# Linear attention block: three x tiles transposed on TensorE, crossbar blocks of 2, 3, 4, 4 tiles, and a state that ends by feature block

## The chip, the cores and the metric

The kernel runs on one core of one Trainium2 chip. The metric is the device time of one execution in microseconds; lower is better.

The core has five engines with a queue each: TensorE (PE in the profile, and PEld for its weight loads), VectorE (DVE), ScalarE (ACT), GpSimd (POOL) and SyncE (SP, which here only starts DMAs). All queues run at the same time, each in its own order, and meet at semaphores.

## The reference

The input x has 2048 rows (tokens) of 640 features, in bf16. There are 32 heads of 20 features.

```python
qkv = (x @ wqkv) split into q, k, v, each [32 heads, 2048, 20]
phi = lambda t: where(t > 0, t + 1, exp(t)) + 1e-6
pq, pk = phi(q), phi(k)
kv  = einsum("bhsd,bhse->bhde", pk, v)      # per head, 20 x 20
z   = einsum("bhsd->bhd", pk)               # sum over tokens
num = einsum("bhqd,bhde->bhqe", pq, kv)
den = einsum("bhqd,bhd->bhq", pq, z) + 1e-6
out = (num / den) as [2048, 640] @ wo
```

## The kernel before

The 2048 tokens are 16 tiles of 128. The 640 features are 5 blocks of 128 (the index c or d in the code). Nothing is recomputed and everything stays in SBUF after one load.

The kernel never forms v. It uses kv = pk^T (x wv) = (x^T pk)^T wv in effect: a state x^T pk of 640 x 640 is summed over the tokens, multiplied by wv, masked to the heads' diagonal blocks, and multiplied by wo. The output is then one matmul of the normalized phi(q) with that product.

The stages are these.

- **Loads and transposes.** k and q need x with the features on the partitions (tile xT). NPE says how many x tiles are transposed on TensorE; the rest are transposed by the DMA crossbar. XCH lists the row ranges: the first NPE entries are single tiles for TensorE, the others are one crossbar DMA each, issued by `load_xT` (L181) on SP's queue. `transpose_x` (L187) does one tile on TensorE: five transposes into two PSUM banks, then one copy per bank to xT, by VectorE or ScalarE. The state matmuls use x untransposed (tile xn, loaded by `load_xn`, L224). `load_wk` (L230) issues the first loads on the SP and ScalarE queues; `load_rest` (L253) queues the q weights, the remaining x tiles, the v weights and wo behind the crossbar DMAs on SP.
- **k.** For every token tile `k_half` (L272) makes two halves of 320 columns over five feature blocks, in two of the eight PSUM banks (tile number modulo 4 picks the pair). `k_phi` (L286) applies phi: Exp on ScalarE (L290), two VectorE instructions (L292, L295), which write pk. The first tiles are interleaved with the TensorE transposes by a short string named order (L557).
- **State.** The state is made in two halves of columns, 360 and 280. In each half, `p_step` (L300) adds one token tile into five banks, 0 to 4, one per feature block of x. `p_out` (L312) copies the five banks to tile pt, by ScalarE (even blocks) and VectorE (odd blocks).
- **Beside the state.** `q_tile` (L324) makes one feature block of phi(q) for 512 tokens: five matmuls of 512 columns (L330), Exp on ScalarE (L338), and VectorE (L344, L352). A variant with `two_act` lets ScalarE do the Relu (L342), so that VectorE's last instruction reads SBUF alone (L349). VectorE sums pk over tiles (z, L358 to L385), `z_finish` (L391) sums over the partitions on TensorE, and GpSimd spreads the sums into head masks (zb, L403).
- **After each half.** `kv_group` (L407) multiplies pt by wv for three groups of 120 features, `kv_mask` (L423) keeps the heads' blocks on VectorE, and the w2 functions (L434 to L465) multiply by wo, copy with ScalarE and rearrange the rows by an SP DMA into w2p.
- **Denominators and output.** `den` (L467) and `den_act` (L482) form the reciprocals for half of the tokens as exp(-ln(den)); `den_spread` (L488) spreads them by four SP DMAs, and `normalize` (L495) multiplies phi(q) by them on VectorE. `out_tile` (L533) makes one output tile in two banks; one copy on ScalarE, one on VectorE, one DMA.

PSUM has eight banks. During the state, banks 0 to 4 hold its five sums, and the list small hands out banks 5, 6, 7 in turn to everything else. Each P.add call states what an instruction reads and writes, and waits follow from it; a p_step is one such call, so all its waits stand ahead of its first matmul.

The order of all work after k is written out by hand in a string (L646). Each letter adds the instructions of one piece, for all engines at once:

```text
p  next state step            o  copy the five banks of a half
q  next q tile                Q  the same, Relu on ScalarE
z  next sum of pk             s  z_finish
k, K  kv group of half 0, 1   0 to 5  w2 of group 0 to 5
i, I  denominators            n  next normalization
T  next output tile
```

The first state steps of tiles 0 and 1 (half 0) stand ahead of the string, and the sixteenth output tile behind it.

Of the kernel before, what the change touches and what calls it, by code (L numbers as in the profile page):

```python
# [82 lines left out]
def bass_standalone__linear_attn_block__prompt_kernel(nc, x, wqkv, wo, out):  # L83
    B, S, D = x.shape
    assert (B, S, D) == (1, 2048, 640)
    H, DH = 32, 20
    NC_ = D // 128
    NT = S // 128
# [5 lines left out]
    PW, PO = (3 * GW, D - 3 * GW), (0, 3 * GW)  # L94

    with contextlib.ExitStack() as ctx:
        es = ctx.enter_context

        def sb(name, cols, dt=BF16):
            return es(nc.sbuf_tensor(name, [128, cols], dt))  # L100

        xT = sb("xT", NC_ * S)
        xn = sb("xn", NT * D)
# [4 lines left out]
        pk = sb("pk", NT * D)  # L108
# [4 lines left out]
        pt = sb("pt", NC_ * D)  # L113
# [20 lines left out]
        P = Plan(nc, es)  # L134

        def bank(b, n=BK, off=0, parts=128):
            return ps[0:parts, BK * b + off:BK * b + off + n]
# [9 lines left out]
        def pool_const():  # L147
# [21 lines left out]
            for lo in (True, False):  # L169
# [1 line left out]
                     0 if lo else DH - 1, 1 if lo else -1, "bm")  # L171


        NPE = 4
        XCH = [(0, 128), (128, 256), (256, 384), (384, 512),
               (512, 896), (896, 1408), (1408, 2048)]

        def xch_of(row):
            return next(i for i, (a, b) in enumerate(XCH) if a <= row < b)

        def load_xT():  # L181
            for i, (a, b) in enumerate(XCH[NPE:]):
                P.add("sp", lambda e, a=a, b=b: e.dma_start_transpose(
                    xT[:, :].rearrange("p (c s) -> p c s", s=S)[:, :, a:b], x[0, a:b, :]),
                    writes=[("xT", NPE + i)], dma=True)

        def transpose_x(st, banks, engs):  # L187
            for (lo, hi), b in zip(((0, 2), (2, NC_)), banks):
                v = bank(b, HALF).bitcast(BF16)

                def mm(e, lo=lo, hi=hi, v=v):
                    for c in range(lo, hi):
                        r = e.transpose(  # L193
                            v[:, 128 * c:128 * c + 128],
                            xn[:, st * D + 128 * c:st * D + 128 * c + 128], ident[:, :])
                    return r
                P.add("pe", mm, reads=xn_keys(st) + ["ident"], writes=[("bank", b)])
            for (lo, hi), b, eng in zip(((0, 2), (2, NC_)), banks, engs):
                dst = xT[:, :].rearrange("p (c s) -> p c s", s=S)[
                    :, lo:hi, 128 * st:128 * st + 128]  # L200
                src = bank(b, HALF).bitcast(BF16).rearrange(
                    "p (c s) -> p c s", s=128)[:, lo:hi, :]
                if eng == "act":
                    P.add("act", lambda e, dst=dst, src=src: e.copy(dst, src),
                          reads=[("bank", b), "table"], writes=[("xT", st, lo)])
                else:
                    P.add("dve", lambda e, dst=dst, src=src: e.tensor_copy(dst, src),  # L207
                          reads=[("bank", b)], writes=[("xT", st, lo)])

        def xT_keys(a, b, cs=range(NC_)):  # L210
            keys = []
            for i, (p, q) in enumerate(XCH):
                if p < b and a < q:
                    keys += [("xT", i)] if i >= NPE else sorted(
                        {("xT", i, 0 if c < 2 else 2) for c in cs})
# [8 lines left out]
        def load_xn(a, b, eng):  # L224
            P.add(eng, lambda e: e.dma_start(
                xn[:, a * D:b * D].rearrange("p (t n) -> p t n", n=D),
                x[0, 128 * a:128 * b, :].rearrange("(t p) n -> p t n", p=128)),
                writes=[("xn", t) for t in range(a, b)], dma=True)

        def load_wk():  # L230
            tl = mybir.InstLoadActFuncSet(
                name=nc.get_next_instruction_name(),
                act_func_set_id=ACT_TABLE_SET_LN_EXP, ins=[], outs=[])
            P.add("act", lambda e: e.add_instruction(tl), writes=["table"])  # L234
            for eng, lo in (("sp", 0), ("act", HALF)):
                P.add(eng, lambda e, lo=lo: e.dma_start(
                    xn[:, lo:lo + HALF], x[0, 0:128, lo:lo + HALF]),
                    writes=[("xn", 0, lo)], dma=True)
            for eng, what in (("sp", "w01 w23 w34 x24"), ("act", "x12 w12 w45")):
                for k in what.split():  # L240
                    a, b = int(k[1]), int(k[2])
                    if k[0] == "x":
                        load_xn(a, b, eng)
                    else:
                        P.add(eng, lambda e, a=a, b=b: e.dma_start(
                            wk[:, a * D:b * D].rearrange("p (c n) -> p c n", n=D),
                            wqkv[128 * a:128 * b, D:2 * D].rearrange("(c p) n -> p c n", p=128)),
                            writes=[("wk", c) for c in range(a, b)], dma=True)

        def xn_keys(t):  # L250
            return [("xn", t)] if t else [("xn", 0, 0), ("xn", 0, HALF)]

        def load_rest():  # L253
            w_cols(wqn, 0, D, 0, "wqn", "sp")
            for a, b in ((4, 8), (8, 12), (12, 16)):
                load_xn(a, b, "sp")
            w_cols(wv, 0, D, 2 * D, "wv", "sp")
            P.add("sp", lambda e: e.dma_start(
                wog[0:GW, 0:5 * D].rearrange("p (g n) -> p g n", n=D),
                wo[0:5 * GW, :].rearrange("(g p) n -> p g n", p=GW)),  # L260
                writes=["wog"], dma=True)
            P.add("sp", lambda e: e.dma_start(
                wog[0:gsz[5], 5 * D:6 * D], wo[5 * GW:D, :]), writes=["wog5"], dma=True)
# [36 lines left out]
        def p_step(h, st, ds=range(NC_)):  # L300

            def mm(e):
                for d in ds:
                    r = e.matmul(  # L304
                        bank(d, PW[h]), xn[:, st * D + 128 * d:st * D + 128 * d + 128],
                        pk[:, st * D + PO[h]:st * D + PO[h] + PW[h]],
                        start=(st == 0), stop=(st == NT - 1))
                return r
            P.add("pe", mm, reads=xn_keys(st) + [("pk", st)],
                  writes=[("bank", d) for d in ds])  # L310

        def p_out(h):  # L312
            for d in range(NC_):
                dst = pt[:, d * D + PO[h]:d * D + PO[h] + PW[h]]
                if d % 2 == 0:
                    P.add("act", lambda e, d=d, dst=dst: e.copy(dst, bank(d, PW[h])),  # L316
                          reads=[("bank", d)], writes=[("pt", d, h)])
                else:
                    P.add("dve", lambda e, d=d, dst=dst: e.tensor_copy(dst, bank(d, PW[h])),
                          reads=[("bank", d)], writes=[("pt", d, h)])  # L320

        nq = [0]

# [230 lines left out]
        warm(6)  # L554
        transpose_x(0, (6, 7), ("dve", "act"))
        warm(1)
        order = "t1 k00 k10 k01 k11 k02 k12 k03 k13 k04 t2 k14 t3"  # L557
        for k in order.split():
            st = int(k[1])
            if k[0] == "t":  # L560
                transpose_x(st, *{1: ((4, 5), ("dve", "act")), 2: ((6, 6), ("dve", "dve")),
                                  3: ((7, 7), ("act", "act"))}[st])
            else:
                for h in range(2):
                    k_half(st, h, (int(k[2]),))
        for st in range(2):
            k_phi(st)
        for st in range(2, NT):
            for cs in ((0, 1), (2, 3, 4)) if st < 4 else (range(NC_),):
                for h in range(2):  # L570
                    k_half(st, h, cs)
            k_phi(st)
# [3 lines left out]
        small = [5, 6, 7]  # L576
# [5 lines left out]
        def next_q(two_act=False):  # L582
            q_tile(*qs.pop(0), take(), two_act)
# [23 lines left out]
            kv_group(0, b)  # L607
            kv_mask(0, b)

        steps = [(0, st) for st in range(2, NT)] + [(1, st) for st in range(NT)]  # L610
        tiles = list(range(NT - 1))

        def pair(st):
            return 2 * ((st + 1) % 4)

        def state_out():
            assert len(steps) in (NT, 0)
            h = 1 if steps == [] else 0
            p_out(h)
            if h:  # L620
                small[:] = [5, 6, 7]

        def late_kv():
            kv_group(1, 4)
# [8 lines left out]
        def next_out():  # L633
            st = tiles.pop(0)
            out_tile(st, pair(st))
            if st == 1:
                small[:] = [1]

        step = {"p": lambda: p_step(*steps.pop(0)), "o": state_out,
                "q": next_q, "Q": lambda: next_q(True), "z": lambda: zst.pop(0)(),  # L640
                "n": lambda: work(1), "s": lambda: z_finish(take()),
                "i": lambda: inverse(0), "I": lambda: inverse(1),
                "k": early_kv, "0": lambda: fold_wo(0), "1": lambda: fold_wo(1),
                "2": lambda: fold_wo(2), "K": late_kv, "3": lambda: late_w2(3),
                "4": lambda: late_w2(4), "5": lambda: late_w2(5), "T": next_out}
        for a in "QzqpzqzppppzpzpQpppQqpzpppoqqkpzzpp1QQp2ppsp0pQipqpppnppnppnonnQKnQn35n4qQqQqqTTnInTnnnTnTnTnTnTTTnnnTTTTT".replace(" ", ""):  # L646
            step[a]()
        assert not (qs or zst or steps or todo or tiles)
        out_last(NT - 1, (0, 1, 2))
# [35 lines left out]
```

## Time and profile before

| | |
|---|---|
| Median of 6 runs | 102.23 us (101.81 to 104.42) |
| Profiled execution, its own time | 101.81 us |
| Its span in the profile | 100.6 us |
| TensorE matmul busy | 97.3 us, 97% of the span |
| VectorE busy | 64.6 us, 64% |
| ScalarE busy | 45.1 us, 45% |
| GpSimd busy | 4.2 us, 4% |
| Granted TensorE clock | 1.000 |

The span runs from the first to the last instruction of the core; the execution's own time has 1.2 us more. Names such as L277 are lines of the kernel. A row of an instruction group gives the busy time, the mean of one in ns, and the idle time of its engine just before. A matmul's row shows more than its share of TensorE's time, since matmuls are pipelined; the chain of waits counts each moment once. That chain starts at the last instruction and goes back, at every step, to what released it.

The stages can be found in time by their lines: TensorE's first k matmul starts at 5.12 us, the first state step at 27.75, the first q tile at 29.27, the first kv group at 48.58 and the second at 66.39, the first output tile at 75.91.

### The profile page before, as it was taken

The numbers are of one execution on the slowest core, as the hardware profiler recorded it, in microseconds if no ns is written. First come the engines' busy times: TensorE is split into PE (matmuls) and PEld (weight loads), VectorE is DVE, ScalarE is ACT, GpSimd is POOL, SyncE is SP. The second block draws the span as 40 slices with busy tenths as digits, with TensorE's granted clock in tenths as the row PEclk, the third lists the DMA queues.
The fourth block names the chain that finished last, engine by engine and source line by source line (L and its number), as shares of the span: only waits on it lengthen the run. The fifth ranks groups of instructions, "written<-read, shape, count | busy, mean of one in ns | idle before, by whom it ended". The sixth has DMA issues, their size and how long they took to land.

```text
span 100.6 us, 1807 instructions
## 1 busy us (share of the span) xinstructions
PE 97.3 (97%) x704; PEld 64.6 (64%) x704; DVE 64.6 (64%) x131; ACT 45.1 (45%) x87; POOL 4.2 (4%) x18
## 2 busy tenths in 40 slices
PE   6899999999999999999999999999999999999992
PEld 2367677777765666566767867855556677777771
DVE  0112999988874999569799423487589518837331
ACT  5115754445526204054439363077984523333222
POOL 6300000000000000000000510000000000000000
DMA  2999999999992000000002222200220234533334
GB/s 59 305 288 180 234 200 213 360 378 366 309 202 49 0 0 0 0 3 0 3 7 61 61 62 43 62 7 0 77 66 0 99 90 117 206 126 125 130 130 130
DMA packets 17076, 11.93 MB, mean 119 GB/s; under 512 B 8621, under 2 KB 17069, under 8 KB 17069
## 3 DMA queue, kind: packets, MB, share of 16 engines
q1 hardware_dynamic: 16349, 11.22, 40.8%
q10 hardware_dynamic: 720, 0.61, 1.8%
q8 instruction: 5, 0.08, 0.3%
q14 instruction: 2, 0.02, 0.1%
HBM read 5.90 MB, written 2.62 MB: 85 GB/s over the span
## 4 chain that ended last, share of the span: by engine, by line
PE 93%; DMA 4%; ACT 0%; DVE 0%; issue 0%
PE ps L277 22%; PE ps L304 22%; PE ps L505 22%; PE ps L330 22%; DMA xn<-in_x_dram 4%; PE ps L436 2%; PE ps L414 2%; PE ps L473 1%; PE ps L193 1%; ACT L234 0%; DVE osb L530 0%; PE ps L395 0%
## 5 line engine op out<-in xcount | busy, mean ns | idle before, releaser
L304 PE MATMUL ps<-pk,xn 128*128 128x360 bf16 (+1 forms) x160 | 23.7, 299 | 0.0
L330 PE MATMUL ps<-xT,wqn 128*128 128x512 bf16 x100 | 23.4, 379 | 0.0
L277 PE MATMUL ps<-wk,xT 128*128 128x320 bf16 x160 | 22.5, 299 | 0.0
L505 PE MATMUL ps<-w2p,pq 128*128 128x320 bf16 (+1 forms) x165 | 22.1, 295 | 0.0
L304 PEld LDWEIGHTS ps<-pk,xn 128*128 128x128 bf16 x160 | 15.4, 98 | 6.9 <-issue 0.2
L505 PEld LDWEIGHTS ps<-w2p,pq 128*128 128x128 bf16 x165 | 15.8, 98 | 6.2 <-issue 0.2
L277 PEld LDWEIGHTS ps<-wk,xT 128*128 128x128 bf16 x160 | 15.3, 98 | 6.3 <-issue 0.3
L338 ACT ACTIVATE eq<-ps 128x512 bf16<-128x512 f32 x20 | 11.9, 598 | 15.2 <-PE ps L330 15.1
L330 PEld LDWEIGHTS ps<-xT,wqn 128*128 128x128 bf16 x100 | 11.7, 118 | 8.3
L290 ACT ACTIVATE ek<-ps 128x640 bf16<-128x640 f32 x16 | 11.1, 709 | 8.2 <-PE ps L277 8.2
L295 DVE SCALAR_TENSOR_TENSOR pk<-ps,ek 128x640 bf16<-128x640 f32 x16 | 13.2, 825 | 0.5
L527 ACT CAST osb<-ps 128x320 bf16<-128x320 f32 (+1 forms) x17 | 7.0, 416 | 13.1 <-PE ps L505 11.8
L530 DVE CAST osb<-ps 128x320 bf16<-128x320 f32 (+1 forms) x16 | 7.6, 477 | 8.0 <-PE ps L505 8.0
L344 DVE TENSOR_SCALAR eq<-eq 128x512 bf16<-128x512 bf16 x20 | 5.8, 292 | 9.9 <-ACT eq L338 9.6
L498 DVE TENSOR_TENSOR pq<-pq,rd 128x512 bf16<-128x512 bf16 x20 | 7.6, 417 | 2.6 <-DMA rd<-rdc 2.6
L352 DVE SCALAR_TENSOR_TENSOR pq<-ps,eq 128x512 bf16<-128x512 f32 x10 | 6.9, 692 | 0.3
L292 DVE TENSOR_SCALAR ek<-ek 128x640 bf16<-128x640 bf16 x16 | 5.2, 323 | 2.8 <-ACT ek L290 2.8
L342 ACT ACTIVATE rq<-ps 128x512 bf16<-128x512 f32 x10 | 5.9, 592 | 0.0
L358 DVE TENSOR_TENSOR za<-pk 128x1280 f32<-128x1280 bf16 x4 | 5.8, 1482 | 0.0
L207 DVE COPY xT<-ps 128x256 bf16<-128x256 bf16 (+1 forms) x4 | 1.1, 305 | 6.7 <-PE ps L193 6.7
L349 DVE TENSOR_TENSOR pq<-eq,rq 128x512 bf16<-128x512 bf16 x10 | 4.3, 425 | 1.7 <-ACT rq L342 1.6
L316 ACT CAST pt<-ps 128x360 bf16<-128x360 f32 (+1 forms) x6 | 2.2, 434 | 6.0 <-PE ps L304 6.0
(40 smaller groups left out, 42.5 us busy)
## 6 DMA issues: line engine op xcount, KB each, us to landing
out_dram<-osb SPq DMA_DIRECT2D x15, 160.0 KB, 1.8
xn<-in_x_dram SPq DMA_DIRECT2D x3, 640.0 KB, 7.9
wqn<-in_wqkv_dram SPq DMA_DIRECT2D x1, 800.0 KB, 5.5
wv<-in_wqkv_dram SPq DMA_DIRECT2D x1, 800.0 KB, 10.5
wog<-in_wo_dram SPq DMA_DIRECT2D x1, 750.0 KB, 13.2
w2p<-w2g SPq DMA_DIRECT2D x5, 150.0 KB
rd<-rdc SPq DMA_DIRECT2D x8, 64.0 KB, 2.1
wk<-in_wqkv_dram SPq DMA_DIRECT2D x3, 160.0 KB, 3.7
```

Source lines behind the costliest of these rows:

```text
L277: r = e.matmul(bank(b + h, HALF), xT[:, c * S + 128 * st:c * S + 128 * st + 128], wk[:, c * D + HALF * h:c * D + HALF * (h + 1)], start=(c ...
L290: P.add("act", lambda e: e.activation(fold(t[:, :]), two_banks(b), ACTF.Exp), reads=banks + ["table"], writes=[("ek", st % 3)])
L295: P.add("dve", lambda e: e.scalar_tensor_tensor(fold(pk[:, st * D:(st + 1) * D]), two_banks(b), 0.0, fold(t[:, :]), ALU.max, ALU.add), rea ...
L304: r = e.matmul(bank(d, PW[h]), xn[:, st * D + 128 * d:st * D + 128 * d + 128], pk[:, st * D + PO[h]:st * D + PO[h] + PW[h]], start=(st == ...
L330: r = e.matmul(bank(b), wqn[:, d * D:(d + 1) * D].rearrange("p (q c) -> p c q", c=NC_)[:, c, :], xT[:, d * S + BK * sbk:d * S + BK * (sbk ...
L338: P.add("act", lambda e: e.activation(t[:, :], bank(b), ACTF.Exp), reads=[("bank", b), "table"], writes=[("eq", i)])
L342: P.add("act", lambda e: e.activation(r[:, :], bank(b), ACTF.Relu), reads=[("bank", b), "table"], writes=[("rq", i)])
L352: P.add("dve", lambda e: e.scalar_tensor_tensor(pq[:, c * S + BK * sbk:c * S + BK * (sbk + 1)], bank(b), 0.0, t[:, :], ALU.max, ALU.add), ...
L498: P.add("dve", lambda e: e.tensor_tensor(v, v, rd[i][:, BK * h:BK * (h + 1)], ALU.mult), reads=[("rd", i, 2 * h), ("rd", i, 2 * h + 1), (" ...
L505: r = e.matmul(bank(b, hi - lo), pq[:, c * S + 128 * st:c * S + 128 * st + 128], w2p[:, c * D + lo:c * D + hi], start=(c == 0), stop=(c == ...
L527: P.add("act", lambda e: e.copy(osb[j][:, lo:hi], bank(b, hi - lo)), reads=[("bank", b)], writes=keys)
L530: P.add("dve", lambda e: e.tensor_copy(osb[j][:, lo:hi], bank(b, hi - lo)), reads=[("bank", b)], writes=keys)
```

## The change

Three things are edited.

First, tile 3 of x is transposed by the crossbar and not on TensorE, so NPE is 3. The crossbar's row ranges become four DMAs of 2, 3, 4 and 4 tiles in place of three of 3, 4 and 5. The early load of untransposed x on SP brings tile 2 alone, and the first later one brings tiles 3 to 7. In the opening string tile 2 is transposed two k pieces earlier, into banks 6 and 7, with one copy on VectorE and one on ScalarE. k tile 3 is made in one go of five blocks, like the later ones.

Second, each state half keeps the order by token tile up to tile 12. The last three tiles are then added feature block by feature block (`p_block`): three matmuls into one bank, which ends that bank's sum, and the copy of that bank right after. There is no letter o any more; a p is either a step of one tile or a block.

Third, the order string is another one, with 34 letters p, 11 Q and 9 q in place of 30, 10 and 10. The z sums stand closer together, two or more Q tiles stand ahead of the first kv group, w2 of group 1 stands amid the blocks of the second half, and w2 of group 4 stands behind one more Q tile.

```diff
-        NPE = 4
-        XCH = [(0, 128), (128, 256), (256, 384), (384, 512),
-               (512, 896), (896, 1408), (1408, 2048)]
+        NPE = 3
+        XCH = [(0, 128), (128, 256), (256, 384),
+               (384, 640), (640, 1024), (1024, 1536), (1536, 2048)]
...
-            for eng, what in (("sp", "w01 w23 w34 x24"), ("act", "x12 w12 w45")):
+            for eng, what in (("sp", "w01 w23 w34 x23"), ("act", "x12 w12 w45")):
...
-            for a, b in ((4, 8), (8, 12), (12, 16)):
+            for a, b in ((3, 8), (8, 12), (12, 16)):
...
-        def p_out(h):
-            for d in range(NC_):
-                dst = ...
+        def p_out(h, d):
+            dst = pt[:, d * D + PO[h]:d * D + PO[h] + PW[h]]
...
-        order = "t1 k00 k10 k01 k11 k02 k12 k03 k13 k04 t2 k14 t3"
+        order = "t1 k00 k10 k01 k11 k02 k12 k03 k13 t2 k04 k14"
...
-                transpose_x(st, *{1: ((4, 5), ("dve", "act")), 2: ((6, 6), ("dve", "dve")),
-                                  3: ((7, 7), ("act", "act"))}[st])
+                transpose_x(st, *{1: ((4, 5), ("dve", "act")), 2: ((6, 7), ("dve", "act"))}[st])
...
-            for cs in ((0, 1), (2, 3, 4)) if st < 4 else (range(NC_),):
+            for cs in ((0, 1), (2, 3, 4)) if st < 3 else (range(NC_),):
...
-        steps = [(0, st) for st in range(2, NT)] + [(1, st) for st in range(NT)]
+        NB = NT - 3
+
+        def p_block(h, d):
+            def mm(e):
+                for st in range(NB, NT):
+                    r = e.matmul(
+                        bank(d, PW[h]), xn[:, st * D + 128 * d:st * D + 128 * d + 128],
+                        pk[:, st * D + PO[h]:st * D + PO[h] + PW[h]],
+                        start=False, stop=(st == NT - 1))
+                return r
+            P.add("pe", mm, reads=[k for st in range(NB, NT) for k in xn_keys(st) + [("pk", st)]],
+                  writes=[("bank", d)])
+            p_out(h, d)
+            if h == 1 and d == NC_ - 1:
+                small[:] = [5, 6, 7]
+
+        def steps_of(h, first):
+            return [lambda st=st: p_step(h, st) for st in range(first, NB)] + [
+                lambda d=d: p_block(h, d) for d in range(NC_)]
+
+        steps = steps_of(0, 2) + steps_of(1, 0)
...
-        for a in "QzqpzqzppppzpzpQpppQqpzpppoqqkpzzpp1QQp2ppsp0pQipqpppnppnppnonnQKnQn35n4qQqQqqTTnInTnnnTnTnTnTnTTTnnnTTTTT".replace(" ", ""):
+        for a in "qzzppzppzzpppqpQppqppppQppzQQkzQpp2zqpQppppsppppi0pqqpppp1npnpnQKnnQn35Qnn4qnqqQQnTTITnTnnTTnnnnTnTTnnTTTTTT".replace(" ", ""):
```

More of the change, by code (lines that the diff above doesn't have):

```diff
@@ L310, in p_step @@
                   writes=[("bank", d) for d in ds])
-        def p_out(h):
-            for d in range(NC_):
[L314 to L320, printed above, removed]
+        def p_out(h, d):
+            dst = pt[:, d * D + PO[h]:d * D + PO[h] + PW[h]]
+            if d % 2 == 0:
+                P.add("act", lambda e: e.copy(dst, bank(d, PW[h])),
+                      reads=[("bank", d)], writes=[("pt", d, h)])
+            else:
+                P.add("dve", lambda e: e.tensor_copy(dst, bank(d, PW[h])),
+                      reads=[("bank", d)], writes=[("pt", d, h)])
         nq = [0]
@@ L614, in pair @@
             return 2 * ((st + 1) % 4)
[L616 to L621, printed above, removed]
         def late_kv():
@@ L637, in next_out @@
                 small[:] = [1]
-        step = {"p": lambda: p_step(*steps.pop(0)), "o": state_out,
+        step = {"p": lambda: steps.pop(0)(),
                 "q": next_q, "Q": lambda: next_q(True), "z": lambda: zst.pop(0)(),
```

## The prediction

> **What bounds the kernel now.** I read the page's busy shares and the chain first, then the stages of the chain, then the waits of TensorE and the issue and landing of the crossbar transposes.
>
> ```profile
> span 100.6 us, 1807 instructions
> PE 97.3 (97%) x704; PEld 64.6 (64%) x704; DVE 64.6 (64%) x131; ACT 45.1 (45%) x87; POOL 4.2 (4%) x18
> PE 93%; DMA 4%; ACT 0%; DVE 0%; issue 0%
> ```
>
> TensorE (PE) is busy 97% and makes up 93% of the chain of waits. A busy share can hide bubbles, so the chain in order of time counts (start us, length us, what):
>
> ```profile
> 1.23 3.56 DMA xn<-in_x_dram
> 4.84 0.45 PE ps L193 x5
> 5.29 2.57 PE ps L277 x18
> 7.86 0.28 PE ps L193 x5
> 8.13 0.27 PE ps L277 x2
> 8.41 0.28 PE ps L193 x5
> 8.69 2.72 PE ps L277 x20
> 11.41 0.04 issue
> 11.45 16.46 PE ps L277 x120
> ...
> 65.22 1.08 PE ps L330 x5
> 66.30 0.09 issue
> 66.39 0.91 PE ps L414 x15
> 67.30 1.21 PE ps L330 x5
> 68.51 1.09 PE ps L436 x6
> 69.60 6.48 PE ps L330 x30
> ```
>
> From 4.84 to 98.62 TensorE almost never stops. A k tile costs 10 x 0.137 = 1.37 us (16.46/120). Excess is small and local: 0.04 ahead of tile 4; 0.09 of waiting ahead of the second kv group and 0.12 in it (0.91 against 0.79 for the first, both 15 matmuls); 0.13 in the q tile after it (1.21 against 1.08); 0.28 in the six w2 matmuls (1.09 against three times the 0.27 of a pair); and 0.15 in the second half's state matmuls (rows that add to 9.67 against 16 x 0.595). So there is about 0.8 us to win there, plus TensorE work that is removed.
>
> The waits of TensorE's weight loads name the owners of the kv and w2 stalls (total us, times, longest):
>
> ```profile
> PEld ps L414 <- DVE pt L319: 0.5, 1, 0.5
> ...
> PEld ps L436 <- DVE kvt L430: 0.3, 1, 0.3
> ```
>
> The timeline of SP's queue (start, issue time) shows the crossbar blocks of 3, 4 and 5 tiles:
>
> ```profile
> 3.13 4.13 SPq L183 DMA_TRANSPOSE xT<-in_x_dram  x1
> ...
> 7.30 3.25 SPq L183 DMA_TRANSPOSE xT<-in_x_dram  x1
> ...
> 10.59 4.10 SPq L183 DMA_TRANSPOSE xT<-in_x_dram  x1
> ```
>
> Their line's own view gives the time to landing, from each start; asked block by block it is 7.1, 6.4 and 7.6, so they land at 10.2, 13.7 and 18.2:
>
> ```profile
> DMA to landing us min/median/max: 6.4/7.1/7.6
> ```
>
> **What the Trainium skill says.** "TensorE: Matmul & The Clock Gate", section Back-to-back issue gap, prices a warm matmul at N/2.4 + 2.5 ns: 136 ns at 320 columns. The trace has 137, so the inner stretches leave nothing to save. "Perfetto Trace Analysis", section Summary: the profiler window per engine type, says that the window of a DMA issued so is descriptor generation, with the data movement hidden. The trace agrees: the first block's issue ends at 7.26, its data lands 2.97 later. "PSUM — Partial Sum Buffer", section Engine vs sequencer instructions: the ScalarE and VectorE queues are strict FIFO; the trace shows it, as the first exp waits at 9.36 behind the transposes' ScalarE copies though its k tile was complete by 8.13. "Perfetto Trace Analysis", section Matmuls, wants matmul groups to rotate over banks so that evacuation overlaps the next group: the edit of the state half does this; in the trace the five copies at the end of the second half come after the last matmul and cost 0.21.
>
> **The change, part by part.**
>
> *Three tiles on TensorE.* One transpose set goes: 5 transposes, a 0.28 us row on the path. With it go a VectorE copy (347 ns) and a ScalarE copy (372 ns); both engines have idle time here. Tile 2's transposes are placed 4 matmuls earlier and use banks 6 and 7. My walk: tile 1's transposes end at 5.29; 16 k matmuls and the 0.11 excess of the 2.57 row (a wait for VectorE's copy of tile 1) end at 7.59; transposes to 7.87; 4 matmuls to 8.42; k tile 2 to 9.79. Tile 2's x block must have landed by 7.59. Before, 320 KB landed at 2.65 + 4.9 = 7.55; now 160 KB does, so no wait. Its copies (0.29 on VectorE, 0.48 on ScalarE) end by about 8.55, while the first two feature blocks of k tile 2 need only the VectorE one at 8.42 and the rest start at 8.97. Hidden.
>
> The first exp can now start near 8.55, 0.8 us sooner. Then bank 0 is free at about 8.55 + 0.71 + 0.32 + 0.83 = 10.4, ahead of tile 4's start at 11.16, and the 0.04 wait goes. On a tile, VectorE spends 0.323 + 0.825 = 1.15, less than TensorE's 1.37.
>
> *Crossbar blocks of 2, 3, 4, 4.* Tile 3 is now needed from the crossbar at 9.79, tile 5 at 12.53, tile 8 at 16.65, tile 12 at 22.1. Two readings of the old blocks give the arrival. (a) Issue sets it: 4 and 5 tiles cost 3.25 and 4.10 us, 0.82 each; the first block paid 4.13 - 2.45 = 1.68 extra; landing comes about 3.1 after the issue. New landings: 3.13 + 1.68 + 1.64 + 3.0 = 9.45, then 12.0, 15.3, 18.8. (b) Landing intervals set it: from the end of the x load, near 7.0, to 10.2, then 3.5 and 4.5 us: about 1.4 + 0.57 per tile, an estimate from the transfer view's 290 GB/s over 164 KB. The x load being 160 KB shorter starts it near 6.6: 9.2, 12.3, 16.0, 19.7. Both clear the needs, by 0.3 to 0.6 at tile 3 and 0.2 to 0.5 at tile 5. If the cost of a block did not depend on its size, it would be late; that is the rival below. I take no stall.
>
> SP is freed 0.9 us later (13 tiles against 12). Behind it stand wqn (landing 20.2, so 21.1, first used about 29), the x blocks, now with tile 3 (last landing 25.6, so about 26.5, first state matmul 27.6 and the late tiles 12 us after), wv and wo (28.7 and 32, used after 47). All hidden.
>
> K then ends 0.32 sooner: 27.59. The ten first state matmuls are as before.
>
> *The rest, counted from the first q tile* (29.43 before). TensorE's work is the same multiset, since each half still has 80 matmuls: a step 0.76 or 0.595, a block of three tiles 0.456 or 0.357, q 1.08. Summed letter by letter both orders reach the second kv group at 36.69 and the first output tile at 45.85. Only waits differ.
>
> First half: blocks end at 13.14, 13.59, 14.05, 15.58, 16.04. The fourth's VectorE copy stands behind a two-ACT q tile whose Relu ends at 16.25: it ends near 17.2. The first kv group needs it at 18.2, the second half's first step (which waits for all five banks) at 20.07. Hidden by a q tile or more; without that cover it would cost 0.5 to 0.6.
>
> Denominators: the z sums now run together (five at a 1.40 cadence, 2.7 to 9.7), and the last one ends near 25.2. VectorE then has a q tile and a Q tile to finish (to 26.8). TensorE's z sums end at 26.89, the copy zc near 27.3, and GpSimd adds 1.70: 29.1. The denominators start at 29.27. The margin is 0.2, where before it was about 0.4. I take no stall, and keep 0 to 0.4 for the range.
>
> Second half: blocks end at 33.91, 34.27, 34.63, 35.25, 35.61, with a w2 pair amid them. ScalarE's two w2 copies (2 x 0.434) delay the last evacuation to 36.2; VectorE's fourth stands behind one normalization (0.417, its reciprocals landed near 33.8) and ends near 35.8. The kv group needs both at 36.69. So the 0.09 + 0.12 of wait there goes. What is late next is the kv mask: it still follows the Q tile's add (near 38.3) and takes 0.50, while w2 asks at 38.56. That stall of 0.2 to 0.3 I leave as it is.
>
> w2 group 4 is moved behind another Q tile. Its ScalarE copy ends near 42.8, SP's issue starts there, and the landing, estimated from the 2.1 of the rd copies, comes at 44.9. The first output tile asks at 45.85 or later: margin 1, down from about 2. In the output loop normalizations hold up VectorE copies until about 54.2 (the new denominators' reciprocals land near 53.3), but those banks are used again at 56.3. Hidden. One Relu more on ScalarE (0.592) and 0.27 less on VectorE meet no bound.
>
> *Sum.* 0.28 + 0.04 + 0.21 = 0.53. The profiled execution took 101.81 (span 100.6, 1.21 around it); it becomes 101.28. The median shown is 102.23, 0.42 above the profiled one; the gain taken from it gives 101.7.
>
> **Rivals.**
>
> *The crossbar takes over the k stage (slower than before).* If a block costs 3.2 to 3.5 us whatever its size, the landings are 10.23, 13.5, 17.0 and 20.5. Tile 3 waits 0.44, tile 5 another 0.53; tile 8 none. Against the gain of 0.53 that is 0.44 lost: 102.7. It decides from the point where both landings are together over 0.53 us late. For it: the first block of 3 tiles landed no sooner after its start than the next of 4 (7.1 and 6.4). Against: the issue grows from 3.25 to 4.10 with one more tile.
>
> *VectorE's order is late at the denominators.* The 0.2 margin is used up and 0.2 to 0.4 is paid; about 102.0. For it: the longest VectorE instructions stand ahead of the last sum. Against: in the old trace successive instructions overlap slightly, so that the queue runs faster than the sum of its rows.
>
> *All small stalls go.* If the mask stall (0.28), the 0.13 after kv and part of the 0.15 vanish too, the gain is about 1.0: 101.2. For it: w2's order has another Q tile between. Against: the mask's place behind the add is unchanged.
>
> **Numbers.** Forecast 0.44, crossbar 0.22, denominators 0.14, all stalls gone 0.15, something unseen 0.05. About 1% is what a measurement of this kernel can tell from no change. Faster by over 1% (under 101.2) is half of the third rival and a tenth of the others: 0.18. Slower by over 1% (over 103.25) needs a stall of 1.6: the crossbar's tail and the unseen, 0.14. Range 100.9 to 102.9.
>
> **What would show it.** Right: 15 transposes in all, no wait ahead of k tile 3 or 5, the denominators close on zb, no wait of the second kv group for pt copies, w2 still about 1.1. Wrong: TensorE waiting for xT between 9 and 13 us, an idle piece ahead of L473, or the span's end moved by more than 1 us.

## The result, and the profile after

The changed kernel takes 101.8 us (median of 33 runs) against 102.32 for the kernel before (70 runs). The ratio is 0.9953, with a 95% interval of 0.9936 to 0.9969: 0.48 us less. The ratio leaves out the few slow executions, the medians take all. The forecast was 0.53 less and 101.7. The profiled execution took 101.53, with a span of 100.1.

The page of the changed kernel, its first rows and the chain's shares:

```profile
span 100.1 us, 1797 instructions
...
PE 96.7 (97%) x699; PEld 64.1 (64%) x699; DVE 63.8 (64%) x130; ACT 45.6 (46%) x87; POOL 4.2 (4%) x18
...
PE 90%; DMA 4%; ACT 2%; DVE 1%; ACTq 0%; issue 0%; DVEq 0%
```

TensorE has five instructions fewer (699 against 704) and stays the bound, but 3% of the chain has passed to ScalarE and VectorE. Where they stand in it is seen in order of time (start us, length us, what):

```profile
1.72 4.03 DMA wk<-in_wqkv_dram
...
5.80 1.81 PE ps L277 x12
7.61 0.28 PE ps L193 x5
7.89 19.56 PE ps L277 x144
27.45 1.52 PE ps L304 x10
...
64.80 1.09 PE ps L329 x5
65.89 0.02 issue
65.92 0.60 ACT eq L337
66.51 0.50 ACT rq L341
...
67.10 0.43 DVE pq L348
67.53 0.33 DVE kvt L429
...
67.90 0.86 PE ps L435 x4
68.76 1.21 PE ps L329 x5
69.97 0.28 PE ps L435 x2
```

(Line numbers after the state's code are lower by one than before: L435 is a w2 matmul, L429 the kv mask, L329 a q tile.)

Two readings. First, the k stage runs without a stop: 144 matmuls in 19.56 us are 135.8 ns each, where before 120 took 137.2. It ends at 27.45, 0.46 sooner than before (27.91), while the first 16 k matmuls ended at nearly the same time (7.61 and 7.59). Second, the wait ahead of the second kv group is gone from the chain, and in its place stands a path through ScalarE's Exp and Relu and VectorE's add to the kv mask, for which the w2 matmuls wait. The waits of the weight loads say the same (total us, times, longest): none for a pt copy is left, and the one for the mask has grown from 0.3 to 0.5.

```profile
PEld ps L435 <- DVE kvt L429: 0.5, 1, 0.5
```

Set beside the kernel before, the gain is all in the opening:

| stage, by the chain | before | after |
|---|---|---|
| end of the first 16 k matmuls (before: 7.86 less two matmuls) | 7.59 | 7.61 |
| end of k | 27.91 | 27.45 |
| end of k to the end of the q tile ahead of the second kv group | 38.39 | 38.44 |
| from there to the first output tile | 9.77 | 9.75 |
| first output tile to the last TensorE instruction | 22.53 | 22.53 |

Single executions differ by more than the effect. In the opening TensorE waits for the second wk block, whose landing varies (4.03 us from its issue here, 5.35 in one experiment). So below, profiles are compared from stage to stage and whole times by ratios.

### The profile page after: what moved, and what is told of

It reads as the page before. It is cut to its first block, busy times and chain, and to the rows that moved or that the text cites. A ratio compares the mean times of both kernels' runs of the same rounds, so it can differ in the third digit from the quotient of the medians.

```text
span 100.1 us, 1797 instructions
## 1 busy us (share of the span) xinstructions
PE 96.7 (97%) x699; PEld 64.1 (64%) x699; DVE 63.8 (64%) x130; ACT 45.6 (46%) x87; POOL 4.2 (4%) x18
## 4 chain that ended last, share of the span: by engine, by line
PE 90%; DMA 4%; ACT 2%; DVE 1%; ACTq 0%; issue 0%; DVEq 0%
PE ps L504 22%; PE ps L277 21%; PE ps L329 21%; PE ps L304 18%; PE ps L613 4%; DMA wk<-in_wqkv_dram 4%; PE ps L435 2%; PE ps L472 1%; PE ps L413 1%; ACT eq L337 1%; ACT rq L341 0%; ACTq L225 0%; DVE pq L348 0%; ACT L234 0%; DVE kvt L429 0%; DVE osb L529 0%
## 5 line engine op out<-in xcount | busy, mean ns | idle before, releaser
L329 PE MATMUL ps<-xT,wqn 128*128 128x512 bf16 x100 | 23.9, 380 | 0.0
L504 PE MATMUL ps<-w2p,pq 128*128 128x320 bf16 (+1 forms) x165 | 22.1, 295 | 0.0
L504 PEld LDWEIGHTS ps<-w2p,pq 128*128 128x128 bf16 x165 | 15.8, 98 | 6.2 <-issue 0.2
L277 PEld LDWEIGHTS ps<-wk,xT 128*128 128x128 bf16 x160 | 15.3, 98 | 6.8 <-DMA wk<-in_wqkv_dram 0.9
L304 PE MATMUL ps<-pk,xn 128*128 128x360 bf16 (+1 forms) x130 | 19.5, 299 | 0.0
L329 PEld LDWEIGHTS ps<-xT,wqn 128*128 128x128 bf16 x100 | 11.5, 118 | 8.0 <-issue 0.3
L304 PEld LDWEIGHTS ps<-pk,xn 128*128 128x128 bf16 x130 | 12.6, 98 | 6.0
L341 ACT ACTIVATE rq<-ps 128x512 bf16<-128x512 f32 x11 | 6.5, 592 | 0.0
L351 DVE SCALAR_TENSOR_TENSOR pq<-ps,eq 128x512 bf16<-128x512 f32 x9 | 6.2, 692 | 0.3
L207 DVE COPY xT<-ps 128x256 bf16<-128x256 bf16 x3 | 0.9, 291 | 6.3 <-PE ps L193 6.3
L613 PE MATMUL ps<-pk,xn 128*128 128x360 bf16 (+1 forms) x30 | 4.7, 299 | 0.0
```

Of the source, the lines that this page charges most:

```text
L277: r = e.matmul(bank(b + h, HALF), xT[:, c * S + 128 * st:c * S + 128 * st + 128], wk[:, c * D + HALF * h:c * D + HALF * (h + 1)], start=(c ...
L304: r = e.matmul(bank(d, PW[h]), xn[:, st * D + 128 * d:st * D + 128 * d + 128], pk[:, st * D + PO[h]:st * D + PO[h] + PW[h]], start=(st == ...
L329: r = e.matmul(bank(b), wqn[:, d * D:(d + 1) * D].rearrange("p (q c) -> p c q", c=NC_)[:, c, :], xT[:, d * S + BK * sbk:d * S + BK * (sbk ...
L341: P.add("act", lambda e: e.activation(r[:, :], bank(b), ACTF.Relu), reads=[("bank", b), "table"], writes=[("rq", i)])
L504: r = e.matmul(bank(b, hi - lo), pq[:, c * S + 128 * st:c * S + 128 * st + 128], w2p[:, c * D + lo:c * D + hi], start=(c == 0), stop=(c == ...
L613: r = e.matmul(bank(d, PW[h]), xn[:, st * D + 128 * d:st * D + 128 * d + 128], pk[:, st * D + PO[h]:st * D + PO[h] + PW[h]], start=False, ...
```

## The experiments

Theory A is the recorded sum: 0.28 + 0.04 in the opening, 0.21 at the state's end. Theory B came from the profile after: the opening brings everything, and the wait ahead of kv has turned into a wait for the mask.

**The opening alone** (e1). The diff's hunks from NPE down to the k loop are put on the kernel before; state ends and the order string stay old.

> The opening alone (three tiles on TensorE, crossbar blocks of 2, 3, 4, 4), with the old order string and the old ends of the state halves. Theory A, the recorded sum: 0.28 for the transposes and 0.04 for the wait ahead of k tile 4 belong to the opening, 0.21 to the state's ends: 0.32 us less than before, ratio 0.997. Theory B, from the trace after: k ends 0.46 sooner and nothing is won after it, so the opening alone brings all of it: 0.46 to 0.50 us less, ratio 0.9953; in its profile k ends near 27.45 and the second kv group still waits for the pt copies.

Ratio 0.9967 (0.9942 to 0.9992). The interval holds both theories; the profile's chain decides, since the wk block landed late and moves all absolute times:

```profile
8.91 0.28 PE ps L193 x5
9.19 19.56 PE ps L277 x144
...
67.14 0.09 issue
67.23 0.91 PE ps L414 x15
```

From the end of the 16 k matmuls to the end of k it takes 28.75 - 8.91 = 19.84 us, as in the changed kernel (27.45 - 7.61 = 19.84) and 0.48 less than before (27.91 - 7.59 = 20.32). The opening is worth 0.48, not 0.32. The kv wait stands at its old 0.09.

**The state ends and the order string alone** (e2): the changed kernel with the old opening.

> The other half alone: the state halves end by feature block and the new order string, with the old opening (four tiles on TensorE, crossbar blocks of 3, 4, 5). Theory A: 0.21 us less than before, ratio 0.998. Theory B: the wait ahead of the second kv group goes, but the wait for the kv mask ahead of the w2 matmuls and one more costly passage between pieces take the same back: 0.0 within 0.1, ratio 1.000.

Ratio 1.0005 (0.9979 to 1.003), which just holds Theory A's 0.998 too; the profile decides. In its chain k ends at 27.82 and the q tile ahead of kv at 66.26, a distance of 38.44; the first output tile follows 9.75 later. Both equal the changed kernel, and from the end of k to the first output tile this is 48.19 us where before has 48.16. Theory B holds. (The blocks of the first half and the new place of the z sums were not tried apart; with everything else of this half they come to nothing within 0.05.)

**The tile-4 wait alone** (e3). Why does the opening bring 0.48 where 0.28 + 0.04 was counted? The edit keeps all 20 transposes:

```diff
-2: ((6, 6), ("dve", "dve")), 3: ((7, 7), ("act", "act"))
+2: ((6, 6), ("act", "act")), 3: ((7, 7), ("dve", "dve"))
```

> Before with one edit: the two copies of x tile 2 go to ScalarE and those of tile 3 to VectorE (the other way round before), so that ScalarE reaches the first exp earlier and bank 0 is free ahead of k tile 4. No transpose is removed. Theory A: the wait is worth the 0.04 that the chain shows, ratio 0.9996. Theory B: a stop of TensorE also costs a refill of its pipeline, of 299 - 136 = 163 ns (the row's duration of one matmul less its cadence), which the chain books as matmul time: 0.20 us less, ratio 0.998; k ends 0.2 sooner, near 27.7.

Ratio 0.9989 (0.9965 to 1.0014), too wide to tell. In its chain the wait is gone:

```profile
8.59 0.28 PE ps L193 x5
8.87 0.27 PE ps L277 x2
9.14 0.28 PE ps L193 x5
9.42 19.11 PE ps L277 x140
```

From the end of the first 18 k matmuls to the end of k it takes 19.93 (28.52 - 8.59) where before took 20.05 (27.91 - 7.86). So 0.12 is won: three times the 0.04 that the chain of before shows as waiting, but not the 0.20 expected. The starts of single matmuls tell why. Before, the first matmul of k tile 4 starts 0.34 us after the one ahead of it:

```profile
11.11 0.30 PE L277 MATMUL ps<-wk,xT 128*128 128x320 bf16 x1
11.45 0.30 PE L277 MATMUL ps<-wk,xT 128*128 128x320 bf16 x1
```

In a full stream that distance is 0.136, so the stop costs 0.20, as Theory B says, and in e3 it is gone. But the edit makes another one. The k matmuls behind the second set of transposes need tile 2's first copy, which is now ScalarE's and takes 0.37 us to 9.27, where VectorE's took 0.29. First before, then e3:

```profile
8.24 0.44 PE L193 MATMUL ps<-ident,xn 128*128 128x128 bf16 x5
8.52 0.31 PE L277 MATMUL ps<-wk,xT 128*128 128x320 bf16 x1
```

```profile
8.90 0.75 ACT L204 COPY xT<-ps 128x256 bf16<-128x256 bf16 x2 [3.09 <-PE ps L193]
8.98 0.44 PE L193 MATMUL ps<-ident,xn 128*128 128x128 bf16 x5
9.33 0.31 PE L277 MATMUL ps<-wk,xT 128*128 128x320 bf16 x1
```

From the transposes' start to the next k matmul it takes 0.28 before and 0.36 in e3. The 0.08 lost there is what is missing from 0.20.

**w2 later** (e4). If w2 waits for the mask, another q tile in between should hide it.

```diff
-npnpnQKnnQn35Qnn4q
+npnpnQKnnQnQ35nn4q
-small[:] = [7, 6, 0, 1]
+small[:] = [6, 7, 0, 1]
```

> After with one edit: the third q tile past the second half's end is made ahead of the w2 matmuls of groups 3 and 5 and not behind them (and the banks handed out next begin with 6), so that the kv mask is ready when w2 asks. Theory B: the wait of 0.23 ahead of w2 and a refill of 0.16 go, 0.3 to 0.4 us under the changed kernel, ratio to before near 0.992. Theory A (what the waits show alone): 0.2 under it, ratio near 0.9935. Rival C: the last w2 rows arrive too late for the first output tile, which waits: no gain over the changed kernel or a loss, ratio 0.995 or more, and an idle piece ahead of the first output matmul.

Ratio 0.9973 (0.9949 to 0.9997), no better than the changed kernel: rival C. The chain shows the first output matmul (L504) waiting for the last w2 rows:

```profile
69.20 0.59 ACT eq L337
69.79 0.49 ACT rq L341
70.28 1.74 ACT w2g L444 x3
...
72.45 3.19 DMA w2p<-w2g
75.63 0.38 issue
76.01 2.88 PE ps L504 x20
```

On ScalarE's queue the w2 copies now stand behind one more Exp and Relu. The last rearranging DMA, the third started within 1.6 us, takes 3.19 us to its completion; I had estimated 2.1.

**The mask first** (e7). The order on TensorE and ScalarE stays; on VectorE the mask is queued ahead of the add that waits for the Relu. The letter X makes the q tile's matmuls, the kv group with its mask, and then the q tile's other instructions.

```diff
+            if between:
+                between()
...
-npnpnQKnnQn35
+npnpnXnnQn35
```

> After with one edit: at the end of the second half the kv mask stands ahead of the VectorE instructions of the q tile made just before the kv group; the order on TensorE and ScalarE is unchanged. If the chain Exp, Relu, VectorE's add, mask is what took back the wait ahead of kv (theory B), w2 no longer waits and 0.23 plus a refill of up to 0.16 go: 0.2 to 0.4 less than the changed kernel, ratio to before 0.992 to 0.9935. If the gain at the state's ends was lost elsewhere, nothing changes: 0.995.

Ratio 0.9919 (0.9888 to 0.995); the interval overlaps that of the changed kernel (0.9936 to 0.9969), so the profile has to tell the size. The chain through ScalarE is gone (L415 is the kv group here, L437 w2; the 0.18 of issue and the x4 behind it are one q tile of five matmuls, of which the trace lacks a record):

```profile
66.20 0.75 PE ps L415 x15
66.95 0.18 issue
67.14 1.03 PE ps L329 x4
68.16 0.65 PE ps L437 x4
68.81 1.21 PE ps L329 x5
70.02 0.27 PE ps L437 x2
```

From the end of the q tile ahead of kv (66.20 here, 65.89 before the edit) to the last w2 matmul it takes 4.09 in place of 4.35.

**Either edit on the kernel before** (e9 the mask first; e10 the second half ending by feature block, with the old order otherwise).

```diff
e9   -ppnonnQKnQn35        +ppnonnXnQn35
e10  -ipqpppnppnppnonnQK   +ipqpppnpppnpppnnnQK
```

> Before with the mask edit alone: the kv mask ahead of the q tile's VectorE instructions, everything else as before. If the mask's chain is the later of two waits in a row (theory B), the kv group still waits for the pt copies (0.09 in the chain, 0.25 with the refill), and the w2 matmuls lose at most 0.15 of their excess, since the kv wait already covered part of it: from the end of the q tile ahead of kv to the last w2 matmul 3.30 us becomes 3.15 to 3.25; ratio 0.998 to 1.000. If the two waits are independent, it becomes 2.9 to 3.0, ratio 0.996.

> Before with one edit: the second half alone ends by feature block, each copied at once, with the rest of the old order. Theory A: the kv wait of 0.21 goes and stays gone, ratio 0.998. Theory B: the wait ahead of the kv group goes, w2 then starts by the mask's chain 2.0 us after the end of that q tile (2.2 before), so at most 0.2 is won up to w2's start and part of it is given back inside w2: 3.30 us of that stretch become 3.10 to 3.25, ratio 0.998 to 1.000.

The ratios are 0.9983 (0.9958 to 1.0009) and 0.9976 (0.9952 to 0.9999), too wide to tell a gain of 0.03 us from one of 0.2; the profiles can. In the chain of the mask edit alone the kv wait stands:

```profile
66.72 0.09 issue
66.81 0.91 PE ps L416 x15
67.72 0.18 issue
67.90 1.03 PE ps L330 x4
68.92 1.06 PE ps L438 x6
```

In that of the blocks alone the mask's chain stands:

```profile
67.95 0.13 DVE pq L349
68.08 0.21 issue
68.30 0.41 DVE kvt L430
68.71 0.04 issue
68.75 1.27 PE ps L436 x6
```

The same stretch makes a table of two by two. The changed kernel and e7 have one more q tile inside it, of which the 1.08 of an undisturbed one is taken off:

| end of the q tile ahead of kv to the last w2 matmul, us | mask behind the add | mask first |
|---|---|---|
| five copies after the half | 3.30 (before) | 3.27 (e9) |
| by feature block | 3.28 (e10); 3.27 (after) | 3.01 (e7) |

Each edit alone brings 0.02 to 0.03, both together 0.29. The other profiles with the same pieces repeat their field within 0.01: 3.30 and 3.29 (e1, e3), 3.26 and 3.27 (the changed kernel again, e2), 3.01 (both runs of e8 below). Both of my ranges for the single edits (3.15 to 3.25, and 3.10 to 3.25) were still too hopeful.

**Crossbar blocks of 5, 4, 4** (e5).

```diff
-               (384, 640), (640, 1024), (1024, 1536), (1536, 2048)]
+               (384, 1024), (1024, 1536), (1536, 2048)]
```

> After with the first two crossbar blocks joined: 5, 4, 4 tiles in place of 2, 3, 4, 4. K tile 3 then waits for the whole first block. If the issue sets the arrival (0.82 to 0.86 us a tile from 3.12, data about 3.5 later), it lands near 10.9 and tile 3, asked for at 9.79, waits about 1.1: ratio to before near 1.006. If the blocks' sizes do not matter (the rival in which a block has a fixed cost), the first block lands near 8.7 to 10.2 as before and the loss over the changed kernel is 0 to 0.4: ratio 0.995 to 0.999.

Ratio 1.0039 (1.0015 to 1.0064): about 0.9 us over the changed kernel, where the rival allowed 0 to 0.4. In its one profile, of 103.67 us, the first block lands 8.7 us after its start, and TensorE waits for it; when it lands in a run of the median's length (102.67) is not shown.

```profile
PEld ps L277 <- DMA xT<-in_x_dram: 1.4, 1, 1.4
```

The first block's arrival does depend on its size, and with 2 tiles in it the transfer stays hidden.

**One tile further** (e6): x tile 2 goes to the crossbar too.

```diff
-        NPE = 3
+        NPE = 2
-               (384, 640), (640, 1024), (1024, 1536), (1536, 2048)]
+               (256, 512), (512, 896), (896, 1408), (1408, 2048)]
```

> After, one step further: x tile 2 goes to the crossbar too (two tiles on TensorE, blocks of 2, 3, 4, 5 tiles, no early load of x tile 2 on SP). Five more transposes go (0.28). The first block starts 0.47 sooner and needs about 5.6, so it lands near 8.2, and k tile 2 asks for it near 8.15: with no wait 0.28 less than the changed kernel, ratio to before 0.9925; with a wait of 0.1 and a refill of 0.16 nothing is won, 0.995; above 0.997 the crossbar bounds the k stage.

Ratio 0.9906 (0.9875 to 0.9937). Its first block starts at 2.64 and lands 5.3 later, at 7.9, and the waits of TensorE's weight loads list no xT. So even tile 2 has no need of TensorE, though it has little to spare: in the second profile of e8 below, where the other loads came sooner, weight loads waited 0.2 for this block, and the matmuls lost 0.05 by their starts.

**Both** (e8, run on two chips, the second time beside the changed kernel).

> Both of the last two edits on after. They touch different stages, so the gains add if both exist: ratio to before near 0.990. If one of them gives nothing, the ratio is that of the other.

> The changed kernel unaltered, beside the next kernel on one chip: ratio to before 0.995, as measured.

> The kernel with both edits (tile 2 to the crossbar, mask ahead of the add) again, to set it against the changed kernel on one chip: ratio to before 0.989 to 0.990, 0.5 to 0.6 us under the changed kernel.

Ratios 0.9894 (0.9852 to 0.9937) and 0.9852 (0.9808 to 0.9897); the changed kernel on the second chip 0.9949 (0.9925 to 0.9973). The medians there are 101.04 (6 runs) and 101.68. This version beats both kernels. Over the changed one it wins 0.6 us by the medians and 1.0 by the ratios, so the size is loose; the parts that the profiles show are 0.28 for five transposes and 0.26 at the mask.

## Why the prediction was right, and two of its terms were not

The forecast's sign, size and range hold, and the transposes' term (0.28) holds. Of the other two terms one was too large (0.21 counted, 0.03 found) and one too small (0.04 counted, 0.20 found). That the sum came out at 0.48 against 0.53 is luck to that extent: the errors cancel.

- *Failed: "the 0.09 + 0.12 of wait there goes".* The wait did go, but it was worth 0.02 to 0.03. The prediction named what is late next, the kv mask behind the add, and then said "that stall of 0.2 to 0.3 I leave as it is", as if it were a length of its own. It is a time: Exp, Relu, add and mask end 1.97 us after the q tile ahead of kv, before (68.27 - 66.30) as after (67.86 - 65.89). When kv starts sooner, w2 waits longer. The mask before, for the groups that w2 takes first:

```profile
67.87 0.40 DVE L430 TENSOR_TENSOR kvt<-ps,bm 120x240 bf16<-120x240 f32 x1
```

  The table of two by two shows it: only with the mask moved as well does the time come out. The prediction also read the stall of before as larger than it was. It took the 0.28 of excess in the six w2 matmuls and the 0.3 that a weight load waited for the mask, but a weight load's wait is not a stop of the matmuls: with the mask early (e9) these six still take 1.06 in place of 1.09. So before, the mask cost 0.03; after, it costs about what the kv wait did.
- *Mis-sized: "the 0.04 wait goes".* The opening was worth 0.48, of which the transposes are 0.28, so 0.20 is left where 0.04 was counted. It is the stop at k tile 4, which by the starts shown under e3 costs 0.34 - 0.136 = 0.20. The chain counts a stop from the end of the row ahead. A row of 320 columns is 299 ns long, but in a full stream the next matmul starts 136 ns after it; the 163 ns between are booked as matmul time (16.46 for 120 before, where 120 x 135.8 is 16.30). The Trainium skill's page "TensorE: Matmul & The Clock Gate", section Single matmul latency, gives (398 + N)/2.4 ns for a lone warm matmul, which is 299 at 320 columns; the row has the same length, but the profile models the ends of matmuls, so the starts are the firmer evidence.
- *On the price of a matmul in a stream.* The prediction took N/2.4 + 2.5 ns from the section Back-to-back issue gap of that page, and with it that nothing is left to save inside the stretches. The section gives that as the gap of an isolated matmul and less for a stream of wide ones, 131 ns at 512 columns. Here the stream itself keeps to the formula: 135.8 ns at 320 columns, and 216 ns at 512 (1.08 for five).
- *Right: the crossbar is hidden, though by more than I gave.* Landings were 8.7, 10.7, 14.5 and 18.4, against my 9.45 or 9.2, 12.0 or 12.3, 15.3 or 16.0, and 18.8 or 19.7; tile 3 was asked for at 9.79. In the other profiles with this opening the first block landed between 8.08 and 9.55, always over 1 us ahead of its use. The extra 1.68 of the old first block did not come with the new one, whose issue took only 1.72:

```profile
3.12 1.72 SPq L183 DMA_TRANSPOSE xT<-in_x_dram  x1
4.89 3.34 SPq L183 DMA_TRANSPOSE xT<-in_x_dram  x1
```

  The rival in which a block's cost does not depend on its size is excluded by the blocks of 5, 4, 4.
- *Right, but close: no wait for the load of tile 2.* In four of the five profiles with this opening the transposes of tile 2 take their 0.28. In that of e4 they take 0.41, since they wait for the load of their x tile.
- *Right: no wait at the denominators.* zc ended 27.1 after the first q tile's start (27.3 was worked out), zb at 57.92, and the first matmul of the denominators starts at 58.24: a margin of 0.3, not 0.2.
- *Right in sign, thin in margin: w2's last rows.* They met the first output tile in time in the changed kernel. Their last DMA was issued at 71.70; with the 3.19 us of e4 it landed near 74.9 (an estimate), 0.6 ahead of the first output matmul at 75.47, where a margin of 1 was worked out. With ScalarE's copies behind one more q tile they came too late (e4).
- The third rival (all small stalls gone) did not happen, but the runs show that part of it could be had: 0.26 at the mask. The 0.13 of the q tile behind kv, which the prediction also counted as stall, is still there in e7, where nothing waits.
- *Slips that change nothing.* Tile 2's transposes moved by one k piece, two matmuls (18 stood ahead of them before, 16 after), not by two pieces and four matmuls; the walk itself counts 16. And the chance of "faster by over 1%" adds to 0.16 by its own rule (half of 0.15 and a tenth of 0.85), not 0.18.

## What to carry to other kernels

When a wait is removed, ask at what time the next one is over, not how long it lasts: here two waits in a row had to be shortened together, and either edit alone brought 0.03 us at most. On an engine whose instructions overlap, price a stop by the starts of the two instructions around it, less their distance in a full stream: 0.20 us here where the chain showed 0.04. And where a transfer must be early, make its first piece small: 2 tiles landed 5.0 to 6.4 us after the start of their issue, the old first block of 3 after 6.6 to 7.2.

## What the runs showed of the hardware that was not expected

- The q tile of five matmuls takes 1.21 us, not 1.08, when it follows the w2 pair of the 40-wide group; it does so with the mask's wait there and with it gone (1.21 in both chains). After a full-width w2 pair, as with group 4, the next 25 q matmuls take 5.40 in all, 0.216 each. The q tile behind the second kv group, whose last matmuls are 40 wide, takes 1.21 too, and the one behind the first, all full width, 1.08.
- The issue of a crossbar block on SP takes 0.86 us a tile when it is first and small (1.72 for 2), yet 3.34 for the 3 tiles behind it and 2.92 for the next 4. The old first block of 3 took 4.13. With the same opening the block of 3 took from 2.49 to 4.12 in five profiles, so part of an issue seems to be waiting; for what, no run shows.
- The rearrangement of w2's rows, 150 KB within SBUF, took 3.19 us from issue to completion as the third of three in a row (e4); 64 KB copies of the reciprocals take 2.1 to 2.2 in the median, and up to 3.8.
